# Windowed attention, token mixing and an MLP: later mixing matmuls, and another split of the weight preparation

## The chip, the cores and the metric

The kernel runs on one core of one Trainium2 chip. A core has a matrix engine (TensorE, PE in the profile), VectorE (DVE), ScalarE (ACT), GpSimd (POOL) and SyncE (SP), which here only issues transfers. Every engine runs its own list of instructions in order and waits on semaphores for the others. The metric is the device time of one execution in microseconds (us); lower is better.

## The reference

Eight batches of 576 tokens, eight heads of 64. Each head attends to a window of 32 tokens; heads 0 to 3 to the nearest 32, heads 4 to 7 to every fourth token of the last 128. The result, 512 values a token, is `x`. Then tokens are mixed within a batch through a rank of 32, and an MLP of 512, 2048 and 512 follows:

```python
x = attention(q, k, v)                     # (8, 576, 512)
h = x.transpose(0, 2, 1) @ U @ V           # U: 576 x 32, V: 32 x 576
u = x + h.transpose(0, 2, 1)
out = u + np.maximum(u @ w_ch1, 0.0) @ w_ch2
```

`U`, `V` and the weights come as 64-bit floats; the kernel turns their words into 32-bit floats on the chip. Products are made of a high and a low part of each operand, so each matrix product is three: high by high, and the two cross products.

## The kernel before, in words

**Tiles and chunks.** The 8 x 576 tokens are 36 tiles of 128. Chunk 0 has four tiles, chunk 1 two, and ten more have three. For each chunk the MLP loops over 16 steps `f` of 128 hidden columns: `layer1(f)` is twelve matmuls into `ph` (L858, three terms of four), ScalarE writes the high part of the relu `hh` (L863), VectorE the low part `hl` (L864), and then `layer2(f - 1)` adds into one `acc` per tile (L882, three matmuls a tile). There are two `ph` buffers, and in chunk 0 one of them serves as the fourth `acc`: there `layer1(f + 1)` can start only when `hl(f)` has been read out of `ph`.

**What stands between.** Attention for later batches and token mixing are items in one list, `queue`, each with a due time in chunks. `slot()` stands behind every fourth matmul of layer 1 and every third of layer 2, and runs the items that are due by then. The order of PE, DVE and ACT is the program's; in chunk 0 that of POOL and SP as well. Items of attention: scores (L362), masking and row maximum on VectorE (`soften`, L376), exponentials on ScalarE (L380), probabilities turned around (`turn`), product (L409), and `place`, which divides and writes into `x` or into `xp` (L441). For the first 18 groups `turn` is a transpose on PE into `ptp` (L386) and a copy out of it by ScalarE (L393).

**Token mixing.** `rest_items(b)` has seven items for a batch: `t_rest` (x times U, 20 matmuls, L491), `t_sum` (a chain: ScalarE copies half of it, L498; VectorE adds, L499; then for each half of the columns ScalarE casts, L503, VectorE subtracts, L504, ScalarE casts again, L505), and five times `mix_rest` (a matmul `m` of `ts_sb`, L513, and an add into `x` on VectorE, L515). For batches 2 to 7 their due times are `REST_AT`, as shares of a burst of attention behind the batch's last group.

**Weights.** In chunk 0 the weights are prepared piece by piece, one piece of w1 and one of w2 per step, by `weight_step()`, called twice a step. A piece passes four stages: ScalarE makes a float of its high words and a number of its low words (L193, L197), VectorE shifts (L201), the low words are added (`add_low`, L203), and `finish` casts to the high part `h` and subtracts on GpSimd to the low part `l` (L210). One call does `finish` for piece i - 3, `add_low` for i - 2 and the first two stages for i - 1. In the kernel before, `add_low` is on GpSimd for w2 and on VectorE for w1; the cast is on VectorE for w2 (L209) and on ScalarE for w1 (L207).

Of the kernel before, what the change touches and what calls it, by code (L numbers as in the profile page):

```python
# [80 lines left out]
HI2 = 2.45  # L81
MIX_AT = 0.735
BURSTS = ((0, 1.31), (5, 2.17), (9, 3.45), (14, 4.95), (18, 6.45), (23, 7.95), (27, 9.45))
REST_AT = (0.36, 0.41) + tuple(0.46 + 0.08 * i for i in range(6))
TURNS = 4
ORDERED = {mybir.EngineType.PE, mybir.EngineType.DVE, mybir.EngineType.Activation, mybir.EngineType.Pool,
           mybir.EngineType.SP}
# [48 lines left out]
def attention_moe_kernel(ctx: ExitStack, tc: tile.TileContext, qk, v0, vv, masks, ident, ut, vt, uv, w1, w2, out):  # L136
    nc = tc.nc
# [12 lines left out]
    def make_w(lo, hi, side):  # L150
        pool = tc.tile_pool(name=f"w{lo}", bufs=1, side=side)
        pool = ctx.enter_context(pool)
        n = hi - lo
        t1 = [pool.tile([P, KC, n * P], F32R, name=f"w1{i}_{lo}") for i in "hl"]
        t2 = [pool.tile([P, n, DM], F32R, name=f"w2{i}_{lo}") for i in "hl"]
        if lo == F_LAST:
            pool.tile([P, PAD], F32, name="pad")
        for f in range(lo, hi):
            fs = slice((f - lo) * P, (f - lo + 1) * P)
            held_w[f] = [t[:, :, fs] for t in t1] + [t[:, f - lo, :] for t in t2]  # L160
# [38 lines left out]
    def narrow_b(parts, v, eng):  # L199
        vi = v.bitcast(I32)  # L200
        nc.vector.tensor_scalar(out=vi, in0=vi, scalar1=3, scalar2=None, op0=ALU.logical_shift_left)  # L201
        for lo, hi, cs in parts:
            eng.tensor_tensor(out=vi[:, cs], in0=vi[:, cs], in1=lo, op=ALU.add)  # L203

    def narrow_c(v, h, l, eng, on_act):
        if on_act:
            nc.scalar.copy(out=h, in_=v)  # L207
        else:
            nc.vector.tensor_copy(out=h, in_=v)  # L209
        eng.tensor_tensor(out=l, in0=v, in1=h.bitcast(F32), op=ALU.subtract)  # L210

    w1v = w1.bitcast(I32).rearrange("(c p) f -> p c f", p=P)
# [23 lines left out]
    def finish_w(f, layer, n):  # L236
        def go(v):
            h, l = held_w[f][2 * layer:2 * layer + 2]
            if layer == 0:
                v = v.rearrange("p (c f) -> p c f", c=KC)  # L240
            narrow_c(v, h, l, nc.gpsimd, layer == 0 and f > 0)
        return go

    pieces = [
# [5 lines left out]
    place_of = {}  # L250
# [2 lines left out]
        place_of[f, layer] = len(pieces)  # L253
        pieces.append((wv, DM, finish_w(f, layer, len(pieces))))
    LATE = place_of[F_LAST, 0]
    w2_places = {n for (f, layer), n in place_of.items() if layer}
    NPIECE = len(pieces)
    at = {}
    sent = {}
# [1 line left out]
    def narrowed(i):  # L261
        narrow_first(i)
        narrow_second(i)
# [16 lines left out]
    def finish(i):  # L280
        pieces[i][2](pipe[i][1])
        finished.add(i)

    def weight_step():
        i = at.get(0, NSMALL + 4)
        at[0] = i + 1
        if NSMALL <= i - 3 < NPIECE and i - 3 not in finished:
            if i - 3 == LATE:
                prep_open.close()
                make_w(F_LAST, FC, "right")  # L290
            finish(i - 3)
        if NSMALL <= i - 2 < NPIECE and i - 2 not in added:
            add_low(i - 2, nc.gpsimd if (i - 2) in w2_places else nc.vector)
        if NSMALL <= i - 1 < NPIECE and i - 1 not in scaled:
            narrowed(i - 1)
        half = LATE
        send(min(NPIECE, i + AHEAD if i + AHEAD <= half else max(half, i + 2)))

    def send(to):
        while NSMALL + len(sent) < to:  # L300
            n = NSMALL + len(sent)
            sent[n] = True
            pipe[n] = fetch64(n)

    def add_low(i, eng):
        narrow_b(*pipe[i], eng)
        added.add(i)
# [75 lines left out]
    def turn_pe(g, p_sb):  # L383
        tp = psum.tile([KB, UNITS, P], F32, tag="ps", name=f"ptp{g}")
        for u in range(UNITS):
            nc.tensor.transpose(out=tp[:, u, :], in_=p_sb[:, u], identity=id_sb)  # L386
        return tp

    def turn(g, part=None):
        p_sb = state[g][0]  # L390
        pt = pts[g % NPT]
        if g < PE_T:
            nc.scalar.copy(out=pt, in_=turn_pe(g, p_sb))  # L393
            return
        r = part
        rs = slice(WIN * r, WIN * (r + 1))
        for k in (r % 2, r % 2 + 1):
            ks = slice(WIN * k, WIN * (k + 1))
            nc.vector.transpose(out=pt[ks, :, rs], in_=p_sb[rs, :, ks])  # L399
# [200 lines left out]
    def attention_items(b):  # L600
# [5 lines left out]
        for k, when in zip(range(lo, hi + 1), whens):  # L606
# [23 lines left out]
            for n, g in enumerate(old):  # L630
# [3 lines left out]
                elif g % NGB == NGB - 1:  # L634
                    ends[g // NGB] = [when + gap * at_ for at_ in REST_AT]
            for n, g in enumerate(new):
                for us in (range(0, 2), range(2, 4)):
                    items.append((when + gap * (0.02 + 0.02 * us[0] + 0.15 * n), lambda g=g, us=us, soft=soft: soft(g, us)))
                for r in range(TURNS) if late else [None]:
                    at_ = 0.45 + 0.2 * n + 0.05 * r if late else 0.42 + 0.26 * n  # L640
                    items.append((when + gap * at_, lambda g=g, r=r: turn(g, r)))
# [192 lines left out]
    for c, tiles in enumerate(CHUNKS):  # L834
# [53 lines left out]
        for f in range(FC):  # L888
            if c == 0 and f == F_MID - 1:
                after_first()  # L890
            if c == 0:
                weight_step()
            if c == NCHUNK - 1 and f == FC - 1:
                order = tc.manual_schedule(engines=ORDERED)
                order.__enter__()
            layer1(f)
            if f < FC - 1:
                slot()
            else:
                for t in more[0:2]:  # L900
                    transp(t)
            if c == 0:
                weight_step()
            if f > 0:
                layer2(f - 1)
                if f < FC - 1:
                    slot()
# [7 lines left out]
        for i, t in enumerate(tiles):  # L915
            x = xt.pop(t)
            n = 2 if t == NTILE - 1 else 1
# [86 lines left out]
```

## Time and profile before

| | |
|---|---|
| three runs | 957.28, 957.63, 960.87 us (median 957.63) |
| profiled execution | 956.64 us, of which the span of the profile 954.9 |
| PE busy | 929.4 us, 97% of the span |
| DVE, ACT, POOL busy | 493.2, 297.7, 74.0 us |
| POOL busy after 160 us | 0 |
| mean granted clock of PE | 0.992 of full speed |

The rows further down come from this execution. A timeline row has the start of an instruction in us from the start of the span, its duration, its engine and line, what it writes and reads, how many like it follow, and in brackets how long its engine had nothing to do before it and what ended that. Matmuls overlap, so their durations are longer than the distance of their starts. In the windows, each engine has its busy time with the number of its instructions, PEclk is the granted clock of PE as a share of full speed.

### The profile page before, as it was taken

How to read it: one execution, taken by the hardware profiler on the slowest of the kernel's cores; microseconds unless marked ns; L12 is line 12 of the kernel's file. 1: busy time of each engine (PE TensorE's matmuls, PEld its weight loads, DVE VectorE, ACT ScalarE, POOL GpSimd, SP SyncE). 2: the span in 40 equal slices, each digit the busy share in tenths (PEclk: the TensorE clock that was granted, in tenths of full speed). 3: DMA queues.
4: the chain of work that ended last, by engine and by line, in shares of the span. 5: the costliest groups of instructions: out<-in, count | busy, mean ns of one | idle time of the engine just before them, and what ended most of it. 6: DMA issues, size and time to landing. Idle time of an engine off the chain costs nothing.

```text
span 954.9 us, 17476 instructions
## 1 busy us (share of the span) xinstructions
PE 929.4 (97%) x6672; PEld 808.1 (85%) x6672; DVE 493.2 (52%) x1677; ACT 297.7 (31%) x930; POOL 74.0 (8%) x67
## 2 busy tenths in 40 slices
PE   9898999998999999999999999999999999999998
PEld 6576778887898889988888978988899888999997
DVE  5665865775546465455545456555744543212211
ACT  6776562333223233223212222223222311111110
POOL 1545561000000000000000000000000000000000
PEclk9999999999999999999999999999999999999999
DMA  9677633532242223132141023222123101011000
GB/s 319 204 224 236 187 102 96 166 92 72 61 109 75 55 67 122 51 108 82 49 115 58 24 66 98 87 78 92 66 70 88 50 23 45 34 27 40 34 1 33
DMA packets 65907, 86.04 MB, mean 90 GB/s; under 512 B 8896, under 2 KB 38144, under 8 KB 65824
## 3 DMA queue, kind: packets, MB, share of 16 engines
q1 hardware_dynamic: 65824, 84.93, 29.8%
q8 instruction: 52, 0.85, 0.4%
q14 instruction: 31, 0.25, 0.1%
HBM read 62.88 MB, written 17.89 MB: 85 GB/s over the span
## 4 chain that ended last, share of the span: by engine, by line
PE 85%; DVE 6%; ACT 4%; issue 2%; POOL 2%; DMA 0%; DVEq 0%; SPq 0%; ACTq 0%; POOLq 0%
PE ph L858 38%; PE acc L882 37%; PE pv L409 4%; PE s L362 3%; ACT p L380 2%; DVE pt L399 1%; PE t L491 1%; PE m L513 1%; POOL v L203 1%; DVE v L203 1%; DVE hl L864 1%; ACT hh L863 1%; DVE p L376 1%; PE ptp L386 1%; PE idle_ps L773 1%
## 5 line engine op out<-in xcount | busy, mean ns | idle before, releaser
L864 DVE SCALAR_TENSOR_TENSOR hl<-ph,hh 128x384 fp32r<-128x384 f32 (+2 forms) x192 | 107.1, 558 | 360.8 <-ACT hh L863 360.3
L863 ACT ACTIVATE hh<-ph 128x384 fp32r<-128x384 f32 (+2 forms) x192 | 93.9, 489 | 472.0 <-PE ph L858 471.9
L882 PE MATMUL acc<-w2h,hh 128*128 128x512 f32 x577 | 220.6, 395 | 0.8 <-ACT hh L863 0.8
L882 PE MATMUL acc<-w2h,hl 128*128 128x512 f32 x577 | 219.1, 392 | 0.4 <-DVE hl L864 0.4
L882 PE MATMUL acc<-w2l,hh 128*128 128x512 f32 x577 | 218.7, 392 | 0.0
L858 PE MATMUL ph<-uth,w1h 128*128 128x384 f32 (+2 forms) x768 | 169.1, 342 | 3.1 <-DVE hl L864 3.1
L858 PE MATMUL ph<-utl,w1h 128*128 128x384 f32 (+2 forms) x768 | 166.7, 339 | 0.0
L858 PE MATMUL ph<-uth,w1l 128*128 128x384 f32 (+2 forms) x768 | 166.2, 338 | 0.0
L858 PEld LDWEIGHTS ph<-uth,w1h 128*128 128x128 f32 x768 | 139.4, 190 | 21.9 <-DVE hl L864 4.4
L380 ACT ACTIVATE p<-p,nmax 128x96 f32<-128x96 f32 x288 | 102.9, 367 | 146.0 <-DVE nmax L376 146.0
L858 PEld LDWEIGHTS ph<-utl,w1h 128*128 128x128 f32 x768 | 134.1, 189 | 4.9 <-issue 1.2
L858 PEld LDWEIGHTS ph<-uth,w1l 128*128 128x128 f32 x768 | 134.5, 189 | 4.1 <-issue 0.4
L399 DVE STREAM_TRANSPOSE pt<-p 32x128 f32<-32x128 f32 x432 | 130.0, 301 | 6.5
L882 PEld LDWEIGHTS acc<-w2h,hl 128*128 128x128 f32 x577 | 108.2, 188 | 24.5 <-DVE hl L864 1.0
L882 PEld LDWEIGHTS acc<-w2h,hh 128*128 128x128 f32 x577 | 107.9, 188 | 19.1 <-ACT hh L863 1.0
L882 PEld LDWEIGHTS acc<-w2l,hh 128*128 128x128 f32 x577 | 108.2, 188 | 17.0 <-issue 0.4
L376 DVE CUSTOM_DVE_ANT_0 p<-s,mask 128x96 f32<-128x96 f32 x288 | 60.0, 252 | 47.7 <-PE s L362 47.3
L409 PEld LDWEIGHTS pv<-v,pt 96*64 96x64 f32 x1152 | 37.5, 137 | 13.4 <-issue 9.0
L380 ACT ACTIVATION_READ_ACCUMULATOR p<-p,nmax 128x1 f32 x252 | 47.1, 187 | 0.0
L409 PE MATMUL pv<-v,pt 96*64 96x64 f32 (+1 forms) x1152 | 43.4, 226 | 1.3 <-ACT pt L651 0.8
L362 PE MATMUL s<-k 64*64 64x96 f32 x1152 | 33.7, 250 | 0.1
L515 DVE TENSOR_TENSOR x<-x,m 128x512 f32<-128x512 f32 (+1 forms) x40 | 27.3, 684 | 6.2 <-PE m L513 5.6
(71 smaller groups left out, 507.4 us busy)
## 6 DMA issues: line engine op xcount, KB each, us to landing
k<-qk SPq DMA_DIRECT2D x64, 288.0 KB, 4.3
raw<-w SPq DMA_DIRECT2D x25, 512.0 KB, 4.3
v<-vv SPq DMA_DIRECT2D x63, 192.0 KB, 3.0
out<-x SPq DMA_DIRECT2D x35, 256.0 KB, 2.1
zd<-z SPq DMA_DIRECT2D x120, 64.0 KB, 1.8
xt<-zd SPq DMA_DIRECT2D x30, 256.0 KB, 2.7
raw<-w SPq DMA_DIRECT2D x14, 256.0 KB, 3.6
x<-xp SPq DMA_DIRECT2D x84, 32.0 KB, 2.5
```

Of the source, the lines that this page charges most:

```text
L203: eng.tensor_tensor(out=vi[:, cs], in0=vi[:, cs], in1=lo, op=ALU.add)
L362: nc.tensor.matmul(sp[r][i * QB:(i + 1) * QB, n, a, :], lhsT=qk_sb[rs, a, i * QB:(i + 1) * QB], rhs=qk_sb[rs, a, P + i * off:P + i * off + ...
L376: nc.vector.tensor_tensor_reduce(out=p_sb[:, u], in0=sp[u % 2][:, u // 2], in1=mask_sb[:, kind], scale=-1.0 / 8.0, scalar=3.0e38, op0=ALU. ...
L380: nc.scalar.activation(out=p_sb[:, u], in_=p_sb[:, u], func=AF.Exp, bias=nmax[:, u:u + 1], scale=-1.0, accum_out=ssums[g][:, u:u + 1] if g ...
L386: nc.tensor.transpose(out=tp[:, u, :], in_=p_sb[:, u], identity=id_sb)
L399: nc.vector.transpose(out=pt[ks, :, rs], in_=p_sb[rs, :, ks])
L409: nc.tensor.matmul(pv[rs, n, u, :], lhsT=pts[g % NPT][:, u, rs], rhs=v[0:KB, i, u, :], start=True, stop=True)
L515: nc.vector.tensor_tensor(out=x, in0=x, in1=mp[rs], op=ALU.add)
L858: nc.tensor.matmul(ph, lhsT=w[:, k, :], rhs=u[:, k, :], start=(n == 0), stop=(n == len(seq) - 1))
L863: nc.scalar.activation(out=hh, in_=ph, func=AF.Relu)
L864: nc.vector.scalar_tensor_tensor(out=hl, in0=ph, scalar=0.0, in1=hh.bitcast(F32), op0=ALU.max, op1=ALU.subtract)
L882: nc.tensor.matmul(acc[i][:, cs], lhsT=h[:, i * P:(i + 1) * P], rhs=w[:, cs], start=(f == 0 and n == 0), stop=(f == FC - 1 and n == 2 and ...
```

## The change

Four edits. The due times `REST_AT` of the token mixing for batches 2 to 7 become 0.34 and 0.38 (from 0.36 and 0.41) for the product and the sum, and start at 0.54 (from 0.46) for the five mixes, 0.08 apart as before. All casts of weights to `h` are on VectorE. All `add_low` are on GpSimd. And the copy of the transposed probabilities is on VectorE.

```diff
-REST_AT = (0.36, 0.41) + tuple(0.46 + 0.08 * i for i in range(6))
+REST_AT = (0.34, 0.38) + tuple(0.54 + 0.08 * i for i in range(5))
...
-    def narrow_c(v, h, l, eng, on_act):
-        if on_act:
-            nc.scalar.copy(out=h, in_=v)
-        else:
-            nc.vector.tensor_copy(out=h, in_=v)
+    def narrow_c(v, h, l, eng):
+        nc.vector.tensor_copy(out=h, in_=v)
         eng.tensor_tensor(out=l, in0=v, in1=h.bitcast(F32), op=ALU.subtract)
...
-            narrow_c(v, h, l, nc.gpsimd, layer == 0 and f > 0)
+            narrow_c(v, h, l, nc.gpsimd)
...
-            add_low(i - 2, nc.gpsimd if (i - 2) in w2_places else nc.vector)
+            add_low(i - 2, nc.gpsimd)
...
         if g < PE_T:
-            nc.scalar.copy(out=pt, in_=turn_pe(g, p_sb))
+            nc.vector.tensor_copy(out=pt, in_=turn_pe(g, p_sb))
             return
```

Line numbers of the changed kernel are three or four smaller from there on. The order of PE in batch 5, before; `t` is the product with U, `ph` layer 1, `acc` layer 2, `m` the first mix:

```order
L491 MATMUL t_6321<-x_4254,us 32x256 x2
L858 MATMUL ph_9_6312<-utl_5872,w1h_1102 128x384 x4
L882 MATMUL acc_0_5905<-w2h_1104,hh_8_6277 128x512
L882 MATMUL acc_0_5905<-w2l_1105,hh_8_6277 128x512
L882 MATMUL acc_0_5905<-w2h_1104,hl_8_6278 128x512
L882 MATMUL acc_1_5906<-w2h_1104,hh_8_6277 128x512
L882 MATMUL acc_1_5906<-w2l_1105,hh_8_6277 128x512
L882 MATMUL acc_1_5906<-w2h_1104,hl_8_6278 128x512
L513 MATMUL m_0_6357<-ts_sb,vs 128x512
```

Six matmuls of layer 2 stand between the product with U's last rows and the first mix, behind one group of layer 1. And now:

```order
L854 MATMUL ph_9_6312<-utl_5872,w1h_1102 128x384 x4
L878 MATMUL acc_0_5905<-w2h_1104,hh_8_6277 128x512
L878 MATMUL acc_0_5905<-w2l_1105,hh_8_6277 128x512
L878 MATMUL acc_0_5905<-w2h_1104,hl_8_6278 128x512
L878 MATMUL acc_1_5906<-w2h_1104,hh_8_6277 128x512
L878 MATMUL acc_1_5906<-w2l_1105,hh_8_6277 128x512
L878 MATMUL acc_1_5906<-w2h_1104,hl_8_6278 128x512
L878 MATMUL acc_2_5907<-w2h_1104,hh_8_6277 128x512
L878 MATMUL acc_2_5907<-w2l_1105,hh_8_6277 128x512
L878 MATMUL acc_2_5907<-w2h_1104,hl_8_6278 128x512
L854 MATMUL ph_10_6362<-uth_5871,w1h_1102 128x384 x4
L509 MATMUL m_0_6367<-ts_sb,vs 128x512
```

The first mix stands three matmuls of layer 2 and a group of layer 1 later; the product with U stands where it did.

VectorE in chunk 0 around `hl` of step 5, before (`v` are pieces of weights between the stages; the row of L203 is the add on VectorE):

```order
L864 SCALAR_TENSOR_TENSOR hl_5_1143<-ph_5_1115,hh_5_1142 128x512
L201 TENSOR_SCALAR v_1120<-v_1120 128x320
L209 CAST w2h_84<-v_1053 128x512
L201 TENSOR_SCALAR v_1110<-v_1110 128x512
L203 ISA v_1110<-raw_975,v_1110 128x1024
L201 TENSOR_SCALAR v_1152<-v_1152 128x512
```

The cast to `w2h`, a shift and the add follow each other. And now, with the copies of probabilities (`pt`) from PSUM and both casts:

```order
L860 SCALAR_TENSOR_TENSOR hl_5_1143<-ph_5_1115,hh_5_1142 128x512
L201 TENSOR_SCALAR v_1120<-v_1120 128x320
L206 CAST w2h_84<-v_1053 128x512
L201 TENSOR_SCALAR v_1110<-v_1110 128x512
L389 COPY pt_77<-ptp_1160 96x512
L206 CAST w1h_1102<-v_1110 128x4x128
L201 TENSOR_SCALAR v_1152<-v_1152 128x512
```

The add is gone from VectorE's list, and the cast to `w1h`, which waits for the same add on GpSimd, stands between two shifts.

VectorE somewhat later, where rows of a group are placed (`x`), before:

```order
L209 CAST w2h_1104<-v_1152 128x512
L201 TENSOR_SCALAR v_1185<-v_1185 128x512
L203 ISA v_1185<-raw_1113,v_1185 128x1024
L417 TENSOR_SCALAR ssum_1287<-sum_1036 128x4
L418 RECIPROCAL ssum_1287<-ssum_1287 128x4
L441 TENSOR_TENSOR x_452<-pv_1196,ssum_1287 64x256
L441 TENSOR_TENSOR x_911<-pv_1196,ssum_1287 64x256
```

The placing stands behind the cast, the shift and the add. And now:

```order
L206 CAST w2h_1104<-v_1152 128x512
L201 TENSOR_SCALAR v_1185<-v_1185 128x512
L413 TENSOR_SCALAR ssum_1287<-sum_1036 128x4
L414 RECIPROCAL ssum_1287<-ssum_1287 128x4
L437 TENSOR_TENSOR x_452<-pv_1196,ssum_1287 64x256
L437 TENSOR_TENSOR x_911<-pv_1196,ssum_1287 64x256
L372 ISA p_1234,nmax_1235<-s_0_1213,mask 128x96
L372 ISA nmax_1235 128x1
```

The placing follows the shift; the cast of the w1 piece stands behind the masks that follow here.

## Rows read from the trace of the kernel before

**Rows 1.** Waits of PE: in total, times, longest, in us
```profile
PE m L513 <- DVE ts_sb L504: 8.6, 4, 2.7
PE ptp L386 <- DVE x L441: 4.1, 1, 4.1
PE ph L858 <- DVE hl L864: 3.1, 2, 2.9
PE ptp L386 <- DVE xp L441: 1.4, 1, 1.4
```

**Rows 2.** Windows of 20 us: busy time by engine, granted clock, DMA
```profile
80.00:100.00 20.00, 15.89 (x124) 12.44 (x117) 11.62 (x42) 11.34 (x33) 8.81 (x8) 0.91 0.72 212
...
240.00:260.00 20.00, 20.00 (x148) 17.91 (x148) 11.58 (x44) 3.90 (x16) 0.00 (x0) 0.92 0.22 62
...
560.00:580.00 20.00, 18.00 (x136) 15.68 (x135) 12.26 (x30) 3.92 (x9) 0.00 (x0) 0.91 0.15 33
```

**Rows 3.** Timeline of PE at the sum and the first mix of batch 5
```profile
558.90 0.97 PE L858 MATMUL ph<-utl,w1h 128*128 128x384 f32 x4
559.71 0.39 PE L882 MATMUL acc<-w2h,hh 128*128 128x512 f32 x1
...
560.86 0.39 PE L882 MATMUL acc<-w2h,hl 128*128 128x512 f32 x1
563.25 0.47 PE L513 MATMUL m<-ts_sb,vs 128*128 128x512 f32 x1 [2.00 <-DVE ts_sb L504]
```

**Rows 4.** Timeline of ACT and DVE there: the chain of the sum
```profile
560.49 0.37 ACT L498 COPY tsum<-t 64x256 f32<-64x256 f32 x1
...
562.69 0.41 DVE L504 TENSOR_TENSOR ts_sb<-tsum,ts_sb 32x256 fp32r<-32x256 f32 x1 [0.43 <-ACT ts_sb L503]
```

**Rows 5.** Timeline of PE: the first mix of batch 2
```profile
238.51 0.47 PE L513 MATMUL m<-ts_sb,vs 128*128 128x512 f32 x1 [2.68 <-DVE ts_sb L504]
```

**Rows 6.** Lines 203, 207, 209, 393: ns min/median/max, first and last start
```profile
L203 DVE CUSTOM_DVE_ANT_0 v<-raw,v x17: 412/1644/1676, 39.7 to 139.8; 128x1024 uint16<-128x1024 uint16 x11, 128x512 uint16<-128x512 uint16 x6
...
L207 ACT CAST w1h<-v x15: 602/621/624, 35.4 to 140.3; 128x512 fp32r<-128x512 f32 x15
...
L209 DVE CAST w2h<-v x16: 417/423/430, 38.9 to 147.0; 128x512 fp32r<-128x512 f32 x16
...
L393 ACT COPY pt<-ptp x9: 564/567/581, 46.1 to 103.9; 96x512 f32<-96x512 f32 x9
```

**Rows 7.** POOL by line and shape: busy us, mean ns, idle before
```profile
L210 POOL TENSOR_TENSOR w2l<-v,w2h 128x512 fp32r<-128x512 f32 x16 | 22.4, 1399 | 15.9 <-DVE w2h L209 15.9
...
L203 POOL TENSOR_TENSOR v<-v,raw 128x512 int32<-128x512 int32 x15 | 19.6, 1309 | 12.4 <-ACT raw L197 12.0 <-DVE v L201 0.4
L203 POOL TENSOR_TENSOR v<-v,raw 128x256 int32<-128x256 int32 x8 | 5.8, 746 | 0.0
```

**Rows 8.** Timeline of DVE in chunk 0: shift, cast, custom add, placing
```profile
77.33 1.11 DVE L201 TENSOR_SCALAR v<-v 128x512 int32<-128x512 int32 x1
...
84.82 0.42 DVE L209 CAST w2h<-v 128x512 fp32r<-128x512 f32 x1
...
85.62 1.64 DVE L203 CUSTOM_DVE_ANT_0 v<-raw,v 128x1024 uint16<-128x1024 uint16 x1
...
87.58 0.86 DVE L441 TENSOR_TENSOR x<-pv,ssum 64x256 f32<-64x256 f32 x2
```

**Rows 9.** Timeline of POOL in chunk 0
```profile
77.22 0.94 POOL L203 TENSOR_TENSOR v<-v,raw 128x320 int32<-128x320 int32 x1 [1.28 <-ACT v L193]
...
132.07 1.41 POOL L210 TENSOR_TENSOR w2l<-v,w2h 128x512 fp32r<-128x512 f32 x1 [0.54 <-DVE w2h L209]
```

**Rows 10.** Timeline of PE: starts of layer 1, steps 0, 11 and 15 of chunk 0
```profile
32.31 1.59 PE L858 MATMUL ph<-uth,w1h 128*128 128x512 f32 x4
...
119.86 0.86 PE L858 MATMUL ph<-uth,w1h 128*128 128x512 f32 x3
...
143.79 1.21 PE L858 MATMUL ph<-uth,w1h 128*128 128x512 f32 x4 [0.19 <-DVE hl L864]
```

More of the change, by code (lines that the diff above doesn't have):

```diff
@@ L255, in attention_moe_kernel @@
     LATE = place_of[F_LAST, 0]
-    w2_places = {n for (f, layer), n in place_of.items() if layer}
     NPIECE = len(pieces)
```

## The prediction

> **What bounds the kernel now.** I read the list of waits of the matrix engine first, because that engine is busy for almost the whole span: what it waits for is nearly all that an edit beside it can give back. Four lines carry the list [rows 1]: 8.6 us in four waits of the mixing matmul (L513) for the last subtraction of the token-mixing sum (L504), 4.1 and 1.4 us in which a transpose of probabilities (L386) waits for VectorE to place an older group's rows (L441), and 3.1 us in which layer 1 (L858) waits for VectorE's `hl` (L864). Together 17.2 us; all else is below 1.3 us each. Second I read the windows of 20 us for the granted clock. Of 47, four are under 1.00; three are shown [rows 2]: 0.91 at 80:100, 0.92 at 240:260, 0.91 at 560:580, and the fourth is 40:60. In each the engine ran for a while at the lower of its two levels (1.2 instead of 2.4 GHz), right behind a wait: 0.09 x 20 = 1.8 us of full-speed work is lost, or 1.6 at 0.92. So two of the waits for the mix cost more than their length. Third, the timelines around the waits, which say what each is made of.
>
> **Mixes one position later.** Take batch 5 [rows 3]. The sum's matmuls end their issue at 558.90, four layer-1 matmuls and six layer-2 matmuls follow, and the first mix, which could have gone about 561.25, starts at 563.25, after 2.00 us of waiting. The chain behind it [rows 4] starts only when ScalarE has done the relu and copies t (560.49) and ends with the last subtraction at 562.69 + 0.41 = 563.10. Nothing in the change shortens that chain. What changes is the cover: three more layer-2 matmuls and one more layer-1 group stand ahead of the mix. A layer-2 matmul of 512 columns costs (560.86 - 559.71)/5 = 0.23 us [rows 3]; four of 384 columns then take 4 x 0.75 x 0.23 = 0.69. Cover gained: 3 x 0.23 + 0.69 = 1.38 us. Batches 3, 5 and 7 have the same order; the list gives 8.6 - 2.68 = 5.9 us for the three [rows 1, 5], so each keeps about 0.6. Gain 3 x 1.38 = 4.1 us.
>
> Batch 2 waits longest, 2.68 us [rows 5]. There the sum also goes one layer-1 group earlier, and its copy now stands ahead of that chunk's relu on ScalarE and its add ahead of `hl` on VectorE. Behind the sum stand three groups and nine matmuls, 3 x 0.69 + 9 x 0.23 = 4.1 us, against a chain of 563.10 - 560.49 = 2.6 us plus the issue. The wait goes whole: 2.7 us. Batches 4 and 6 show no wait now, and get more cover. The mixes themselves are as many as before; the later ones still come before the transposes that read their rows. Sum of the mixes: 4.1 + 2.7 = 6.8 us.
>
> Two of these waits (2.68 and the 2.00 of batch 5) are followed by the lower clock, the other two, of nearly 2.0, are not: at this length it is not certain either way. At 0.6 or nothing I expect no drop: the 1.4 us wait of the transposes is followed by none either. That is 1.6 + 1.8 = 3.4 us.
>
> **Chunk 0: adds from VectorE to GpSimd, casts and copies to VectorE.** Counts: VectorE loses 17 instructions of L203 (11 whole, median 1.64, and 6 halves), ScalarE loses 15 casts of 0.62 and 9 copies of 0.57 [rows 6], some 14 us. VectorE gains 15 casts at 0.42 and 9 copies out of PSUM. GpSimd gains 11 x 1.31 + 6 x 0.75 = 18.9 us [rows 7]. A copy out of PSUM of this shape is not shown on VectorE: 0.42 (its cast of 128x512) [rows 6] and 1.11 (a shift of that shape beside a GpSimd add) [rows 8] bound it, 4 to 10 us for nine; I take 0.6, near ScalarE's 0.57. ScalarE and VectorE have idle time in this stage, so only what ends a wait of the matrix engine counts.
>
> *The transposes' waits.* The custom add stands in VectorE's queue straight ahead of the placing of rows: 85.62 to 87.26 the add, 87.58 to 88.44 the placing [rows 8], and only then the transpose that has waited 4.1 us [rows 1]. In the new order the placing follows the shift, and the cast that waits for GpSimd comes behind the masks. That takes 1.6 us from in front of the placing. The cast of the weight piece before it, however, now waits for an add on GpSimd, which keeps part of it: I take 1.2 (bounds -0.5 and 1.6), so some 2.9 us of that wait stays, and with it the lower clock. The 1.4 us wait [rows 1] has the same build with less behind it: gone, 1.4. The wait of 2.9 us for `hl` [rows 1] stays: ahead of it on ScalarE stand exponentials whose masks are now behind the cast that waits for GpSimd, so what ScalarE loses there is not the last thing. Gain 2.6.
>
> *The new chain.* GpSimd now does, per 128 hidden columns, an add, a subtraction, an add and a subtraction, and before each subtraction it waits 0.54 us for VectorE's cast [rows 9]. That is 2 x (1.31 + 0.54) + 1.40 + 1.30 = 6.4 us, where the 1.30 is the add's price for want of another row [rows 7]. The matrix engine needs (143.79 - 119.86)/4 = 5.98 us for that work late in the chunk [rows 10]; earlier steps are longer, since the attention stands in them. So GpSimd falls behind only over the last four or five steps, by 0.4 each, 0.7 where the adds come in halves: 2 to 3 us. VectorE's first cast stands right behind `hl`, the second ends 0.54 + 1.40 + 1.31 + 0.42 = 3.7 us later and a shift of 0.42 follows; of 5.98 us that leaves 1.9 before the next `hl` is late. I charge 0.3 (bounds 0 and 3).
>
> The Trainium skill speaks against the edit: GPSIMD Engine Reference, section Engine selection, would keep an elementwise operation of two inputs on VectorE, GpSimd being about half as fast. This trace disagrees for this add: 1.31 on GpSimd, 1.64 for VectorE's custom form of as many words [rows 6, 7]. Had the rule held, an add would take some 3.3 us (an estimate from it), the cycle 10 us against (143.79 - 32.31)/15 = 7.4 of an average step [rows 10], and sixteen steps would end 40 us later, near 985. With 15 adds of that size in the trace at 1.31 it gets no chance beyond that of the slower case below.
>
> *Contention.* A shift on VectorE took 1.11 us when it began at 77.33, in an add that GpSimd ran from 77.22 to 78.16 [rows 8, 9], against 0.42 for a cast of that size [rows 6]: it ended 0.3 us after the add. With 17 more adds on GpSimd, each could hold up one such instruction by 0.7: 12 us of VectorE's time at the most, little of it ahead of a waiting transpose, because the casts wait for the add anyhow. Zero in the sum, up to 3 us in the range. The Trainium skill (SBUF — State Buffer, section Who interferes with whom) has the same as a rule: the two engines share a pair of ports, and the second to come waits for the whole instruction of the first. By it the hold would be up to 1.3 us each, 22 us of VectorE's time.
>
> **Sum.** Against the profiled run's own 956.64 us: -6.8 (mixes) -3.4 (clock behind two of them) -2.6 +0.3 (chunk 0) = -12.5, 944.1. That run lies 0.99 below the median of 957.63, so the forecast for a median is 945.
>
> **Rivals.**
> The clock does not come back: the waits shrink, but the lower level appears behind other waits, as it does at 80:100 and 40:60 now. For: 1.93 to 2.00 us shows both outcomes. Against: nothing over 0.7 stays at a mix. 945 + 3.4 = 948.5.
>
> Chunk 0 gives more: the wait of 4.1 us falls to 1.2 as VectorE and ScalarE run ahead, and its drop of clock goes: 945 - 1.7 - 1.8 = 941.5, or 939 if that of `hl` shrinks also.
>
> GpSimd becomes the bound of chunk 0: the cycle is 7.5 us rather than 6.4, by contention on both sides. It falls behind by 1.5 us in each of the last five steps and by some in the middle; some 8 us are lost and the removed waits come back: 950 to 957. For: the cycle then fills the 7.4 us of an average step. Against: the measured rows, 6.4 us a cycle.
>
> Slower than before: VectorE runs in order, and 15 of its casts now wait for GpSimd. From the start of one cast to the end of the next it is those 3.7 us, where the custom add was done 2.44 us after the cast began (84.82 + 2.44 = 87.26 [rows 8]). If masks, placing and `hl` stand behind it every time and the matrix engine waits each time, that is 16 x 1.27 = 20 us: 956.6 - 10.2 + 20 = 966.8, or 967.8 as a median. It decides from some 1.0 us lost per 128 columns. For: at two of the early places the cast does stand straight ahead of masks. Against: elsewhere the placing and masks stand between the two casts, and late in the chunk only `hl` is behind it, with time to spare.
>
> **How the numbers follow.** Forecast (943 to 947) 0.50; clock not back (947 to 950) 0.18; chunk 0 gives more (938 to 943) 0.12; GpSimd the bound (950 to 957) 0.14; slower 0.06. What this kernel's measurement can tell from no change is about 0.5%, 4.8 us: below 952.8 is faster. Of the case in which GpSimd bounds, a little under half lies below it: faster 0.80 + 0.06 = 0.86, same 0.08, slower 0.06. The range 938.5 to 951.5 leaves out the slower case, most of GpSimd's, and the tail of the better chunk 0, some 0.19. The likeliest case alone is 943 to 947.
>
> **What would show it.** Right: the list of waits has no mix over 0.8 us and batch 2 is missing from it; 240:260 and 560:580 are at 1.00; layer 1 of chunk 1 starts some 2 us before 153; GpSimd's subtractions wait about 0.54 for VectorE. Wrong: a mix wait of 1.5 or more, meaning that the chain moved with the mix; a lower clock in a new window; VectorE waiting for GpSimd's adds for over 25 us with layer 1 waiting for `hl` at the end of chunk 0; or GpSimd's adds and VectorE's shifts well over 1.3 and 0.42.

## The result and the profile after

Three runs gave 947.23, 948.92 and 949.48 us: a median of 948.92 against 957.63, a ratio of 0.9895 with an interval of 0.9857 to 0.9933. Six more runs later had a median of 949.46, a ratio of 0.9907 (0.9884 to 0.9930). So it is faster by about 9 us, or 1%, where 12.6 us were forecast. The profiled run took 947.23 us, its span 945.5.

The list of waits of PE in the changed kernel (engine, line, what it waited for: in total, times, longest, us):

```profile
PE ph L854 <- DVE hl L860: 4.8, 4, 3.0
PE ptp L382 <- DVE x L437: 3.7, 1, 3.7
PE m L509 <- DVE ts_sb L500: 1.8, 3, 0.6
PE ptp L382 <- DVE xp L437: 1.6, 1, 1.6
```

Against [rows 1] the mixes went from 8.6 to 1.8 us. The transposes did not get what was forecast: 3.7 and 1.6 where 4.1 and 1.4 stood, and `hl` has two new waits. The windows that were at the lower clock [rows 2], now (busy time of PE, its weight loads, DVE, ACT and POOL, granted clock, DMA):

```profile
80.00:100.00 20.00, 16.29 (x112) 12.83 (x111) 11.76 (x43) 9.92 (x34) 10.56 (x9) 0.91 0.80 240
...
240.00:260.00 20.00, 20.00 (x155) 17.84 (x155) 11.64 (x42) 4.96 (x20) 0.00 (x0) 1.00 0.29 83
...
560.00:580.00 20.00, 20.00 (x156) 17.78 (x155) 12.42 (x45) 5.20 (x21) 0.00 (x0) 1.00 0.41 112
```

Both windows behind a mix are at full clock; the one behind the wait of a transpose is not. Batch 5's first mix, which waited 2.00 us [rows 3], in the timeline of PE:

```profile
558.17 0.47 PE L509 MATMUL m<-ts_sb,vs 128*128 128x512 f32 x1 [0.63 <-DVE ts_sb L500]
```

**Two stretches.** All kernels below are compared by two stretches of PE's timeline that have the same work in each. A runs from the first layer-1 matmul (32.31 us in [rows 10]) to the one matmul of layer 2 in chunk 1 that waits for `hh`; B from there to the last matmul. Their ends in the kernel before, and in the changed one:

```profile
157.82 0.50 PE L882 MATMUL acc<-w2h,hh 128*128 128x512 f32 x1 [0.78 <-ACT hh L863]
...
950.66 0.28 PE L882 MATMUL acc<-w2h,hl 128*128 128x256 f32 x1
```

```profile
31.77 1.59 PE L854 MATMUL ph<-uth,w1h 128*128 128x512 f32 x4
...
158.62 0.50 PE L878 MATMUL acc<-w2h,hh 128*128 128x512 f32 x1 [1.05 <-ACT hh L859]
...
941.23 0.28 PE L878 MATMUL acc<-w2h,hl 128*128 128x256 f32 x1
```

A took 157.82 - 32.31 = 125.5 us and now 126.9; B 792.8 and now 782.6. The whole gain is in B, where the mixes are; chunk 0 lost. It lost more than 1.3 us, because the execution before had two windows at the lower clock in A (40:60 and 80:100, 0.91 each) and the changed one had one. A window at 0.91 loses 0.09 x 20 = 1.8 us; without that, A is 121.9 before and 125.1 after. This count is rough: for the changed kernel run again (e12 below), which has the same two windows at the lower clock as the kernel before, it gives 124.4. The loss is then 2.5 to 3.2 us.

**What chunk 0 lost.** In front of every placing stands an add of 1e-9 to the sums, 128x4, L417 before and L413 now. Its rows from 30 to 160 us by line (count, ns min/median/max), before and then after:

```profile
L417 DVE TENSOR_SCALAR ssum<-sum x9: 156/158/165, 54.6 to 107.8; 128x4 f32<-128x4 f32 x9
```

```profile
L413 DVE TENSOR_SCALAR ssum<-sum x9: 158/906/1268, 52.5 to 107.0; 128x4 f32<-128x4 f32 x9
```

An add of four elements a partition takes up to 1.27 us. The timelines of DVE and of POOL say what it waits for (the changed kernel):

```profile
83.26 0.42 DVE L206 CAST w2h<-v 128x512 fp32r<-128x512 f32 x1
83.60 0.42 DVE L201 TENSOR_SCALAR v<-v 128x512 int32<-128x512 int32 x1
83.93 1.24 DVE L413 TENSOR_SCALAR ssum<-sum 128x4 f32<-128x4 f32 x1
85.20 0.18 DVE L414 RECIPROCAL ssum<-ssum 128x4 f32<-128x4 f32 x1
85.42 0.86 DVE L437 TENSOR_TENSOR x<-pv,ssum 64x256 f32<-64x256 f32 x2
```

```profile
66.32 1.42 POOL L207 TENSOR_TENSOR w2l<-v,w2h 128x512 fp32r<-128x512 f32 x1 [0.54 <-DVE w2h L206]
...
83.76 1.38 POOL L207 TENSOR_TENSOR w2l<-v,w2h 128x512 fp32r<-128x512 f32 x1 [1.76 <-DVE w2h L206]
```

The add begins at 83.93, GpSimd's subtraction runs to 83.76 + 1.38 = 85.14, the add ends at 85.17. The one at 66.49 took 1.27 and ended at 67.76; the subtraction there ended at 67.74. Five of the nine adds meet GpSimd in this way, four for 1.24 to 1.27 us and one for 0.91.

Before the change, the custom add of 1.64 us stood ahead of the small add [rows 8]. The same subtraction and the small add, before (POOL, then DVE):

```profile
85.33 1.39 POOL L210 TENSOR_TENSOR w2l<-v,w2h 128x512 fp32r<-128x512 f32 x1 [1.76 <-DVE w2h L209]
```

```profile
87.18 0.16 DVE L417 TENSOR_SCALAR ssum<-sum 128x4 f32<-128x4 f32 x1
```

The subtraction was over at 86.72, so the small add met nothing. But the custom add had waited in its place: it began at 85.62, during the subtraction, and ended at 87.26, 0.54 us after it. All eleven whole custom adds of chunk 0 begin during a subtraction and end 0.54 to 0.56 us after its end. Late in the chunk the adds come in two halves of one shape, of which the first meets the subtraction and the second does not. A first and a second half, each with the subtraction there:

```profile
125.96 1.41 POOL L210 TENSOR_TENSOR w2l<-v,w2h 128x512 fp32r<-128x512 f32 x1 [2.93 <-DVE w2h L209]
138.15 1.41 POOL L210 TENSOR_TENSOR w2l<-v,w2h 128x512 fp32r<-128x512 f32 x1 [0.54 <-DVE w2h L209]
```

```profile
126.25 1.40 DVE L203 CUSTOM_DVE_ANT_0 v<-raw,v 128x512 uint16<-128x512 uint16 x1
139.76 0.41 DVE L203 CUSTOM_DVE_ANT_0 v<-raw,v 128x512 uint16<-128x512 uint16 x1
```

So of the 1.64 us some 1.1 were a wait for GpSimd. The custom add is gone from VectorE's list, and its wait has passed to the small add.

### The profile page after: what moved, and what is told of

It reads as the page before. It is cut to its first block, busy times and chain, and to the rows that moved or that the text cites. A ratio compares the mean times of both kernels' runs of the same rounds, so it can differ in the third digit from the quotient of the medians.

```text
span 945.5 us, 17486 instructions
## 1 busy us (share of the span) xinstructions
PE 925.8 (98%) x6672; PEld 804.4 (85%) x6672; DVE 485.1 (51%) x1684; ACT 285.9 (30%) x906; POOL 93.6 (10%) x84
## 4 chain that ended last, share of the span: by engine, by line
PE 81%; DVE 6%; ACT 3%; POOL 3%; DMA 3%; issue 2%; SPq 1%; DVEq 0%; POOLq 0%; ACTq 0%
PE ph L854 37%; PE acc L878 36%; PE pv L405 3%; PE s L358 2%; POOL v L203 2%; DMA raw<-w 1%; ACT p L376 1%; PE t L487 1%; DVE pt L395 1%; PE m L509 1%; DVE hl L860 1%; DVE v L201 1%; POOL w2l L207 1%; ACT hh L859 1%; DMA k<-qk 1%
## 5 line engine op out<-in xcount | busy, mean ns | idle before, releaser
L854 PE MATMUL ph<-uth,w1h 128*128 128x384 f32 (+2 forms) x768 | 167.1, 339 | 4.9 <-DVE hl L860 4.8
L854 PEld LDWEIGHTS ph<-uth,w1h 128*128 128x128 f32 x768 | 137.5, 188 | 24.2 <-DVE hl L860 6.4
L203 POOL TENSOR_TENSOR v<-v,raw 128x512 int32<-128x512 int32 (+2 forms) x41 | 45.1, 1108 | 11.9 <-ACT raw L197 10.9
```

Of the source, the lines that this page charges most:

```text
L854: nc.tensor.matmul(ph, lhsT=w[:, k, :], rhs=u[:, k, :], start=(n == 0), stop=(n == len(seq) - 1))
```

## The experiments

Each kernel was timed beside the kernel before on the same chip; times are medians, ratios are to the kernel before beside it. A and B, from the profiled run, are as above; "A at full clock" has 1.8 us taken off for each window at 0.91 (3.4 for one at 0.83), good to about 0.7 us by the two rows of the changed kernel.

| kernel | us | ratio to before, interval | A | A at full clock | B |
|---|---|---|---|---|---|
| before | 957.63 | 1 | 125.5 | 121.9 | 792.8 |
| changed | 948.92 | 0.9895, 0.9857 to 0.9933 | 126.9 | 125.1 | 782.6 |
| e12_after_again | 949.46 | 0.9907, 0.9884 to 0.9930 | 128.0 | 124.4 | 782.6 |
| e1_mixes | 947.60 | 0.9884, 0.9867 to 0.9901 | 127.2 | 122.0 | 782.6 |
| e2_chunk0 | 959.57 | 1.0019, 1.0006 to 1.0033 | 127.9 | 124.3 | 792.9 |
| e3_no_eps | 941.24 | 0.9820, 0.9804 to 0.9837 | 121.4 | 119.6 | 780.8 |
| e4_pt_act | 948.19 | 0.9899, 0.9882 to 0.9917 | 127.0 | 123.6 | 782.6 |
| e5_add_dve | 948.93 | 0.9892, 0.9872 to 0.9912 | 128.5 | 123.3 | 782.6 |
| e6_cast_act | 956.35 | 0.9980, 0.9967 to 0.9993 | 135.2 | 128.0 | 782.6 |
| e8_mixes_eps | 943.81 | 0.9843, 0.9820 to 0.9866 | 124.8 | 121.2 | 780.8 |
| e9_eps_later | 938.74 | 0.9796, 0.9774 to 0.9817 | 121.5 | 119.7 | 778.7 |
| e10_best_pt_act | 940.21 | 0.9812, 0.9789 to 0.9836 | 121.7 | 119.9 | 778.7 |
| e11_add_behind | 943.41 | 0.9850, 0.9825 to 0.9875 | 123.9 | 120.3 | 781.4 |

**Mixes alone, chunk 0 alone.** The kernel before with the one line, and the changed kernel with the old line:

```diff
-REST_AT = (0.36, 0.41) + tuple(0.46 + 0.08 * i for i in range(6))
+REST_AT = (0.34, 0.38) + tuple(0.54 + 0.08 * i for i in range(5))
```

e1_mixes. 

> The kernel before with the new due times of the mixes alone. Theory A (the gain is all in the mixes and the clock behind them; the other three edits give nothing net): 946 to 949 us, as the whole change; the waits of L513 fall from 8.6 to about 1.8 us, chunk 0 keeps its waits. Theory B (the terms as forecast: mixes 10.2, chunk 0 2.3): 947.4 us. Theory C (the edits of chunk 0 give a part of the gain worth 3 us or more): 951 us or more.

e2_chunk0. 

> The changed kernel with the old due times of the mixes: only the edits of chunk 0. Theory A: 957 to 959 us, no change against before, chunk 1 starting its second step within 1 us of before. Theory B (forecast): 955.3 us. Theory C: 953 us or less.

Measured 947.60 and 959.57. Theory A holds for the mixes: they alone give the whole gain. For chunk 0 it was a little kind: the three edits together are slower than nothing, by 0.19%, some 1.8 us, with an interval that leaves out 1. A is 2.4 us longer there than in the kernel before, with as many windows at the lower clock. e1 came out as low as it did although its profiled run had the lower clock in two windows of chunk 0, one of them at 0.83:

```profile
60.00:80.00 20.00, 17.84 (x152) 13.99 (x152) 13.23 (x38) 14.28 (x41) 11.42 (x11) 0.91 0.65 195
80.00:100.00 20.00, 15.73 (x124) 12.48 (x120) 10.80 (x34) 10.87 (x30) 8.48 (x8) 0.83 0.67 200
```

**Without the small add.** A sum of exponentials is at least 1, so in 32 bits the add of 1e-9 changes nothing. In the changed kernel:

```diff
-        nc.vector.tensor_scalar(out=ssum, in0=sums, scalar1=1e-9, scalar2=None, op0=ALU.add)
-        nc.vector.reciprocal(out=ssum, in_=ssum)
+        nc.vector.reciprocal(out=ssum, in_=sums)
```

e3_no_eps. 

> The changed kernel without the add of 1e-9 to the sums of the exponentials ahead of their reciprocal (each sum is at least 1, so in 32 bits the sum is the same). Theory A (that add of 128x4 took 1.24 to 1.27 us at 66.5 and 83.9 because it waited for the end of GpSimd's subtraction, and this is what took the place of the custom add): the two transposes' waits fall by 1.1 us each, 3.7 to about 2.6 and 1.6 to about 0.5; 2 to 4 us faster than the changed kernel. Rival D (the reciprocal behind it waits for GpSimd just as long, or the placing itself does): the waits stay at 3.7 and 1.6 and the time stays. Rival E (what the placing waits for is the cast behind GpSimd's add, not the lock): waits within 0.3 of the changed kernel's.

Measured 941.24, 7.7 us under the changed kernel: more than theory A had asked for. Waits of PE, then DVE and POOL at the same place:

```profile
PE ph L853 <- DVE hl L859: 3.3, 2, 3.0
PE ptp L382 <- DVE x L436: 2.0, 1, 2.0
PE m L508 <- DVE ts_sb L499: 1.8, 3, 0.6
```

```profile
83.76 0.42 DVE L206 CAST w2h<-v 128x512 fp32r<-128x512 f32 x1
84.10 0.42 DVE L201 TENSOR_SCALAR v<-v 128x512 int32<-128x512 int32 x1
84.43 0.17 DVE L413 RECIPROCAL ssum<-sum 128x4 f32<-128x4 f32 x1
84.64 0.86 DVE L436 TENSOR_TENSOR x<-pv,ssum 64x256 f32<-64x256 f32 x2
```

```profile
84.26 1.38 POOL L207 TENSOR_TENSOR w2l<-v,w2h 128x512 fp32r<-128x512 f32 x1 [1.50 <-DVE w2h L206]
```

The reciprocal of the same 128x4 runs in the middle of the subtraction, in 0.17 us, and the placing behind it in its usual time. The transposes' waits fall from 3.7 to 2.0 and from 1.6 to none, and of the new waits for `hl` 0.4 us is left. Rival D falls: what takes the add's place does not wait. Rival E would have left the waits where they were. A is 5.5 us shorter; B is 1.8 us shorter, where the add is gone ahead of the later groups too. Two waits of PE behind VectorE, 0.4 us at 181 and 0.5 at 208, are gone there; the rest is not traced.

**The same add where nobody waits for it.**

```diff
+        if b > 0:
+            nc.vector.tensor_scalar(out=sums, in0=sums, scalar1=1e-9, scalar2=None, op0=ALU.add)
         if moves and b > 0:
```

e11_add_behind. 

> The changed kernel with the reciprocal taken from the sums as they are, and the same add of 1e-9 to the 128x4 sums done behind the placing of rows, where nobody needs its result. As many instructions as in the changed kernel. Theory A (the add waits for GpSimd, and costs by what stands behind it): some of the adds still take 0.9 to 1.3 us, but the transposes' waits are near those without the add (2.0 and none, against 3.7 and 1.6), 941.5 to 944.5 us. Rival D (it is the number of instructions on VectorE, not the wait): 947.5 to 949.5 us. If the adds there are short, the lock's length is shown only by the kernels in which it stands ahead.

Measured 943.41, 6.0 us under the changed kernel beside it (e12) with as many adds of sums in the attention of batch 1 and later (those of batch 0 are left out). Its wait of PE for a placing, and one add that still waits for GpSimd, on DVE:

```profile
PE ptp L382 <- DVE x L436: 2.8, 1, 2.8
```

```profile
68.27 0.73 DVE L440 TENSOR_SCALAR sum<-sum 128x4 f32<-128x4 f32 x1
```

The time is within theory A's, 4 us below rival D's. Only one of the nine adds of chunk 0 is over 0.4 us, though, where 0.9 to 1.3 was expected of some, and the remaining wait is 2.8, not 2.0. So most of the cost comes from where the add stands; the place also decides whether it meets GpSimd, and this kernel does not tell the two apart.

e12_after_again. 

> The changed kernel once more, beside the two others: 947.5 to 949.5 us, four adds of 128x4 at 1.2 to 1.3 us.

 It came out so, at 949.46, with a fifth add of 0.83 us (0.91 in the first profiled run).

**The other three edits, one taken back at a time.** In the changed kernel:

```diff
 # e4_pt_act
-            nc.vector.tensor_copy(out=pt, in_=turn_pe(g, p_sb))
+            nc.scalar.copy(out=pt, in_=turn_pe(g, p_sb))
 # e5_add_dve
-            add_low(i - 2, nc.gpsimd)
+            add_low(i - 2, nc.gpsimd if (i - 2) in w2_places else nc.vector)
 # e6_cast_act
-            narrow_c(v, h, l, nc.gpsimd)
+            narrow_c(v, h, l, nc.gpsimd, layer == 0 and f > 0)
```

e4_pt_act. 

> The changed kernel with the copy of the transposed probabilities back on ScalarE (0.57 us there, 0.68 on VectorE). Theory A (this edit is hidden): within 1 us of the changed kernel. Rival F (the copies on VectorE delay hl and the placing): 1 to 3 us faster than the changed kernel. Rival G (it is what relieves ScalarE's queue): 1 us or more slower.

e5_add_dve. 

> The changed kernel with the adds of w1 pieces back on VectorE; casts and copies stay on VectorE. Theory A (the lock: the custom add fills the time in which GpSimd subtracts, so the 128x4 add behind it meets no lock): its rows are at 0.16 to 0.17 again, the end of chunk 0 has no wait for hl, 946 to 949 us, no better than the mixes alone (947.6). Rival H (GpSimd's longer chain is what costs; without it the casts and copies on VectorE pay): 943 to 945.

e6_cast_act. 

> The changed kernel with the casts of w1 back on ScalarE, the adds on GpSimd: VectorE no longer waits in order for GpSimd's adds of w1 (21.7 us of waits in the changed kernel). Theory A (the lock): the 128x4 add still takes 1.24 to 1.27 us where it meets a subtraction, 947 to 950 us. Rival E (the casts that wait for GpSimd in VectorE's order cost the time): 943 to 946.

The copies: 948.19, hidden, as theory A had it. The adds: 948.93, no change, so neither H nor a gain; but not all of theory A. The add was at 0.15 to 0.17 in six of its nine places, and in three it met GpSimd again (two of the six and one of the three, rows of DVE):

```profile
68.01 0.16 DVE L414 TENSOR_SCALAR ssum<-sum 128x4 f32<-128x4 f32 x1
69.46 0.16 DVE L414 TENSOR_SCALAR ssum<-sum 128x4 f32<-128x4 f32 x1
81.80 1.27 DVE L414 TENSOR_SCALAR ssum<-sum 128x4 f32<-128x4 f32 x1
```

The transposes there wait 5.1 and 2.4 us, longer than in the changed kernel, and a wait of 0.8 for `hl` is left late in chunk 0. So the small add is not all that delays the placing: the custom adds, with their own waits, stand on VectorE again beside all the casts.

The casts: 956.35, 7.4 us slower than the changed kernel, which neither theory expected, and which refutes E. The waits, of PE and then of ACT:

```profile
PE ph L857 <- DVE hl L863: 7.4, 3, 3.8
PE ptp L385 <- DVE x L440: 4.2, 1, 4.2
PE ptp L385 <- DVE xp L440: 2.4, 1, 2.4
```

```profile
ACT w1h L207 <- POOL v L203: 29.5, 11, 3.6
```

On ScalarE the casts wait 29.5 us for GpSimd's adds; in the changed kernel VectorE waits 21.7 us for them. The relu and the exponentials stand behind them on ScalarE, and the waits of PE for `hl` and the placing are longer than in the changed kernel, 7.4, 4.2 and 2.4 us against 4.8, 3.7 and 1.6. With the adds on GpSimd the casts are better off ScalarE: these two edits belong together.

**Without the small add, but with chunk 0 as before; and the mixes later still.** The same edit on e1_mixes, and in e3_no_eps `0.62` in place of `0.54` in `REST_AT`.

e8_mixes_eps. 

> The kernel before with the new due times of the mixes and without the 128x4 add of 1e-9. Theory A: there the add stands behind the custom add and meets no lock (0.16 us in the kernel before), so leaving it out is worth 0.2 us a group: 945 to 948 us against 947.6 with the mixes alone. Rival I (the add is worth the same wherever it stands, so 7.7 us go here too): 940 to 942.

e9_eps_later. 

> The changed kernel without the 128x4 add, and the mixes one more position later (0.62 in place of 0.54). The three waits of 0.6 us at the first mixes go, nothing else: 939.0 to 940.0 us against 941.24. Rival J (the later mixes push the last one against the transposes that read its rows): 941 or more, with a new wait there.

e8: 943.81, 3.8 us under e1, between the two expectations. The columns say why: B is 1.8 us shorter, as in e3, and A at full clock only 0.8 (4.8 to 5.5 in e3, against the two runs of the changed kernel); the rest is the lower clock, by the windows 5.2 us of A in e1's profiled run and 3.6 in e8's. So in chunk 0 the add costs little where the custom add has waited ahead of it, as theory A says; that it also cost 1.8 us in the later chunks, where GpSimd does nothing, it had left out. e3 against e8 is what the three edits of chunk 0 are worth with the add out of the way: 941.24 against 943.81, and 1.6 us of A. The intervals of these two ratios overlap, so that gain is likely but not shown.

e9: 938.74, a little under the 939.0 to 940.0 expected. The list of waits has no mix left, B is 2.1 us shorter than e3's, and no new wait came at the transposes. It has the lowest median, 2.0% under the kernel before beside it. e10, which puts the copies back on ScalarE in it, is no faster:

e10_best_pt_act. 

> The best version so far (changed kernel, no add of 1e-9, mixes from 0.62) with the copies of transposed probabilities back on ScalarE. With the lock out of the way: within 1 us of 938.74 if this edit is hidden; 1 to 2 us faster if the copies hold up VectorE's queue (0.68 us each against 0.57); slower if ScalarE's relu then comes late.

 Measured 940.21 (938.37 to 943.06); A and B are those of e9 within 0.2 us. The median is 1.5 us above e9's, with ranges that overlap; in the profiled run, at 943.06 the longest of the five, the excess lies ahead of A, whose first matmul starts at 36.1 us where e9's starts at 32.4.

## Why the prediction came out as it did

The time lies in the range, 3.9 us above its point, and the difference is one part of the sum, chunk 0. It lies where the prediction put the rival of a clock that does not come back (947 to 950, 0.18), but both windows behind a mix did come back. So the likeliest case, 943 to 947, missed, and the number fell into a rival's band for a reason that is not that rival's: luck, as far as the band goes.

*The mixes.* Forecast 6.8 us of waits and 3.4 of clock, 10.2. B measured 792.8 - 782.6 = 10.2, and 782.6 in all five kernels with the new due times that keep the add ahead of the placing. The waits of L513 fell from 8.6 to 1.8, that is by 6.8, with 0.63 left in batch 5 where 0.6 was worked out, and the two windows behind them are at 1.00. Counting what stands between the product and the mix, and leaving the chain as long as it was, gave the number.

*The new chain on GpSimd.* Forecast 6.4 us a cycle, 0.4 to 0.7 lost each over the last steps, 0.3 charged. POOL's timeline late in chunk 0:

```profile
131.82 1.41 POOL L207 TENSOR_TENSOR w2l<-v,w2h 128x512 fp32r<-128x512 f32 x1 [0.54 <-DVE w2h L206]
133.19 1.45 POOL L203 TENSOR_TENSOR v<-v,raw 128x256 int32<-128x256 int32 x2
135.17 1.41 POOL L207 TENSOR_TENSOR w1l<-v,w1h 128x512 fp32r<-128x512 f32 x1 [0.54 <-DVE w1h L206]
136.55 1.45 POOL L203 TENSOR_TENSOR v<-v,raw 128x256 int32<-128x256 int32 x2
138.54 1.41 POOL L207 TENSOR_TENSOR w2l<-v,w2h 128x512 fp32r<-128x512 f32 x1 [0.54 <-DVE w2h L206]
```

From subtraction to subtraction it is 138.54 - 131.82 = 6.7 us, with adds in halves: the cycle was right. What it cost was 1.8 us, in waits for `hl` of 0.16, 0.97 and 0.69 us, against 0.19 before; e3, with the same chain, has 0.4. The two longer ones, on PE:

```profile
124.73 1.20 PE L854 MATMUL ph<-uth,w1h 128*128 128x512 f32 x4 [0.97 <-DVE hl L860]
143.44 1.21 PE L854 MATMUL ph<-uth,w1h 128*128 128x512 f32 x4 [0.69 <-DVE hl L860]
```

So most of this term too came with the small add. By what way is not shown: the last small add of chunk 0 stands at 107 us, ahead of all three waits.

*The transposes' waits.* This is the step that failed: "That takes 1.6 us from in front of the placing", for a gain of 2.6. The two waits went from 4.1 and 1.4 to 3.7 and 1.6, a gain of 0.2. The 1.64 us were read as the custom add's own length, but 1.1 of them were its wait for GpSimd's subtraction, and that wait stayed. From the start of the cast to the placing it was 87.58 - 84.82 = 2.76 us before, 85.42 - 83.26 = 2.16 in the changed kernel, and 84.64 - 83.76 = 0.88 without the small add. So the edits took 0.6 us from in front of the placing, and 1.3 more would have gone without the small add.

The part on contention had the effect and its size (0.7 to 1.3 us a time, on VectorE instructions that begin while GpSimd runs) and then put zero in the sum. It looked at shifts and casts beside GpSimd's new adds, and not at what stands beside the subtractions that were there before. The instruction that paid was a small one, and it stood exactly ahead of the placings: four times 1.1 us and once 0.75, and A 2.5 to 3.2 us longer at full clock instead of 2.3 shorter. Without the small add the same edits have A at 119.6, which is 2.3 shorter than before; 0.8 of that came in the old split of the work, too (e1 to e8).

The Trainium skill (SBUF — State Buffer, section Who interferes with whom) counts `tensor_scalar` among the VectorE instructions that can take the pair of ports shared with GpSimd when their operands meet certain conditions, and has the second of the two engines blocked until the first is done. The rows agree, 1.24 us for 128x4, ending 0.03 us after GpSimd. The list there does not name the reciprocal; here it did not wait.

*The add on either engine.* The prediction compared 1.31 us on GpSimd with 1.64 on VectorE and concluded that this trace disagrees with the Trainium skill (GPSIMD Engine Reference, section Engine selection). That reading was wrong, since the 1.64 hold the wait. Half a piece took 0.41 us on VectorE with GpSimd at rest and takes 0.75 on GpSimd [rows 7], 1.8 times as long, near what the page says. The cycle in the sum is not touched by this, for it goes by GpSimd's own 1.31.

*The rivals.* GpSimd as the bound did not come about, nor did the slower case: VectorE waits 30.9 us for GpSimd's adds in its 32 casts, and PE's waits for `hl` late in chunk 0 come to 1.8 us. That is one of the prediction's signs of being wrong, over 25 us with layer 1 waiting at the end of the chunk, and it did come. Of its signs of being right, the one for chunk 0 failed: chunk 1 was to start some 2 us before 153. Its first group does start at 151.78, but ahead of matmuls of chunk 0's layer 2 that stood before it, and its first matmul that waits for `hh` stands at 158.62 where it stood at 157.82. The signs for the mixes all came. The copies of probabilities took 0.68 us each on VectorE where 0.6 was taken, and are hidden (e4, e10).

## What to carry to other kernels

When an instruction is taken from one of two engines that hold each other up, find out first how much of its time is a wait: look for the same shape with and without the neighbour at work (1.40 and 0.41 us here). Such a wait need not go with the instruction. The next one on that engine can run into the neighbour instead, and a tiny one can wait as long as a big one. Read its place in front of the critical wait, not its size. And to hide a chain whose length is fixed, count the matmuls between its first input and its first use; that count gave the 6.8 us of waits to within 0.1 us.

## What the runs showed of the hardware

The clock is not settled by the length of a wait. Behind the wait of 2.95 us for `hl` at about 45 us the window 40:60 was at 1.00 in the changed kernel and at 0.91 in the same kernel run again. At the transposes it fell to 0.91 behind 2.8 us (e11), stayed at 1.00 behind 2.0 (e3, e9), and fell in e1 behind 2.2. Of the two equal waits of 2.00 us at first mixes with the old due times, the later was followed by a window at 0.91 in the kernel before, and the earlier in e2. So a wait of 2 to 3 us costs its length and sometimes 1.8 us more.

A subtraction on GpSimd that begins during a shift on VectorE seems to take longer too, by less: those of w1 took 1388 ns in the mean, now that VectorE's shift follows the cast that they wait for, and 1303 before, when the cast was ScalarE's. With that cast back on ScalarE (e6) it is 1291. That the shift is the reason is read from the order of the rows, and no run has the cast on VectorE without the shift.

An instruction on VectorE that is held up by a running one on GpSimd shows the wait as its own duration, not as idle time in front of it: 1.24 us for an add of 128x4 that takes 0.16 alone, 1.40 for half a custom add that takes 0.41.
